# Loading q, k and v as f16 through GpSimd's DMA queue, with seven-product groups in chunks 3 to 5 and a new table of times

## The chip, the core and the metric

The kernel runs on one core of a Trainium2 chip. The metric is the time of one execution on the device in microseconds, in which smaller is better. The engines are called by the profile's names: PE (TensorE, matmuls), DVE (VectorE), ACT (ScalarE), POOL (GpSimd), SP (SyncE, which here only starts DMAs).

## The reference

Attention over 8 batches and 8 heads of 576 tokens, 64 numbers per head, without a softmax, followed by a two-layer network over all 4608 tokens.

```python
theta = np.pi / 2.0 * pos / S
def phi(x, c, s):
    r = np.maximum(x, 0.0)
    return np.concatenate([r * c, r * s], axis=-1)
q_p = phi(q, cos_w, sin_w); k_p = phi(k, cos_w, sin_w)
kv = np.einsum('bhsf,bhsd->bhfd', k_p, v)
z = np.sum(k_p, axis=2)
num = np.einsum('bhsf,bhfd->bhsd', q_p, kv)
den = np.einsum('bhsf,bhf->bhs', q_p, z)[..., None] + 1e-06
attn = num / den                       # then x: 4608 tokens x 512
h = x @ w_in                           # 512 x 2048
g = h * np.cos(h)
out = g @ w_out                        # 2048 x 512
```

Inputs and output are f32; PE multiplies f16.

## The kernel before

**Tiling.** The 576 tokens of a batch are four tiles of 128 and a rest of 64. The 64 left over from each batch are collected into a ninth piece of 512 tokens. So the network runs over nine chunks of 512 tokens: chunk c is batch c for c below 8, and chunk 8 holds the rests.

**Attention of a batch.** `load` brings q, k and v into `raw["q"]`, `raw["k"]`, `raw["v"]` (in the profile qm, km, vm; 128 partitions, 8 heads, 5 tiles, 64 numbers, f32) by two DMAs each, with 5 and with 4 tokens a piece (1280 and 1024 bytes). `prep` (L346 on ACT, L347 on DVE) takes the positive part, multiplies it with the cosine or sine of the position and writes f16 into `KQ`: 18 or 20 of these a batch. `cast_v` (L360, L361, L362) puts v in f16 into `V1` beside a column of ones. `kv` (L373) makes the 128 x 65 products of k and v for each head. q is transposed, for the first two batches on PE (`q_pe`, L402) and later by a DMA (`q_dma`, L412). `num` (L435, L451 to L455) multiplies, divides by the denominator and writes x in f16; x is transposed on PE (L475) or by a DMA (L485).

**Layer 1 of a chunk** multiplies 512 tokens with the 512 x 2048 weights and applies h cos(h). Chunks 0 and 1 do it in halves of tokens (L529). From chunk 2 on there are four groups of four column blocks each. A plain group (`layer1_plain`, L561) has 16 matmuls of 512 columns into four PSUM banks, and for each bank `gate`: a cosine on ACT (L502) and a multiply on DVE (L504). A seven-product group (`layer1_fast`, L667) makes the same result by a scheme of Strassen's kind, from sums of tokens' halves (`layer1_sums`, L624) and sums of weights (`w_in_sums`, L603): seven products of four matmuls of 256 columns. Partial results are put together outside PE: three copies on ACT (L675) and three adds on DVE (L679) into the f32 tiles Y, U and Z, a `gate` for Y and one for the bank that ends last, and `out2`, a double cosine (L690) and a double multiply (L696) over U and Z together. Gates of Y and double multiplies may run on DVE or POOL.

`FAST1 = {3:2,4:2,5:2,6:4,7:4,8:4}` (L568) says how many of a chunk's four groups are of the seven-product kind: none in chunk 2, two in chunks 3 to 5, all in 6 to 8.

**Layer 2** (`layer2`, L861, for chunks from 1 on; `layer2_plain`, L786, for chunk 0) is a seven-product scheme over the whole chunk. Its results go through the f32 tiles `ost` (L872, L883) to the output by `store`: DMAs from POOL's queue (L732, L749), some of them adding to what lies there (L745, L819).

**The order.** Nothing is scheduled while the kernel runs. Each piece of work is added to `Plan` as a step with what it reads and writes. `Plan.run` sorts all 1363 steps by a table of times, `STARTS` (units of 10 ns), and puts each on the engine that the string `ENGS` names (P, A, D, G for POOL, S for SP). Each engine runs its steps in that order, and a step waits for the semaphores of what it needs. So a step that waits holds up all that stands behind it on its engine. Steps marked `port=True` (preparations, casts of v, multiplies with a choice of DVE and POOL, sums between SBUF tiles) wait for each other across DVE and POOL as well, in the order of the table:

```python
if s["port"] and s["on"] in "DG":
    if last is not None and last[0] != s["on"]:
        tc.add_manual_dep(ins.ins, last[1].ins.name, SYNC, reason="shared port")
    last = (s["on"], ins)
```

**The queues.** SP starts the loads of q, k and v and the transposing DMAs. POOL starts the loads of the weights, which cast f32 to f16 on the way, and the stores, beside its own casts and multiplies. ACT starts two loads of constants and some of the last stores.

In the first stages 28 and then 17 matmuls on constant data (`warm`, L945) fill PE's time until batch 0 has arrived. In the last two chunks the tiles of q, k and v are free, and `layer1_fast` uses them as further buffers for Y, U, Z and for the sums of tokens.

Of the kernel before, what the change touches and what calls it, by code (L numbers as in the profile page):

```python
# [16 lines left out]

STARTS = (
# [166 lines left out]
def kernel(  # L185
# [42 lines left out]
    def sb(name, shape, dt=F16):  # L228
        return pool.tile(shape, dt, name=name)
# [897 lines left out]
```

## Time and profile before

| | |
|---|---|
| runs of the kernel | 281.53, 282.29 and 1005.16 us, median 282.29 |
| span of the profiled execution, first to last instruction | 279.7 us |
| busy in the span: PE, DVE, ACT, POOL | 97%, 85%, 75%, 30% |
| granted PE clock | full (1.000) |
| DMA moved | 58.03 MB, 207 GB/s over the span |
| SP's queue, POOL's queue: bytes moved | 39.99 MB, 17.04 MB |
| chain that ended last: PE, ACT, DVE | 92%, 3%, 2% |
| PE's matmuls by part: layer 2 (L861), layer 1 in sevens (L667), plain (L561), halves (L529) | 896, 504, 160, 256 |

The median of the runs is 2.6 us above the profiled span. "Busy" counts an engine's instructions and not the DMAs that it starts, save on POOL, where the writing of descriptors shows as busy. The time of a group of instructions is given as the mean of one; matmuls follow each other closer than their own length, since they are pipelined.

### The profile page before, as it was taken

Reading aid. Unit: us, or ns where it says so; the run is one execution under the profiler, and the core shown is the slowest. Engines: PE = TensorE matmul, PEld = TensorE weight load, DVE = VectorE, ACT = ScalarE, POOL = GpSimd, SP = SyncE. Lnnn points to the kernel's source line nnn. Section 1 sums busy time; section 2 is a strip of 40 time slices with the busy share of each in tenths; the row PEclk is TensorE's granted clock in tenths of the full one; section 3 lists DMA queues with packets and bytes.
Section 4 is the critical chain, followed back from the end, with each engine's and each line's share of the span. In section 5 each row is a group of like instructions: output and inputs, shape, how many; then the busy total and the mean of one; then the engine's idle time right before and its main releaser. Section 6 shows DMA issues by size and latency. Waiting matters only on the chain.

```text
span 279.7 us, 6825 instructions
## 1 busy us (share of the span) xinstructions
PE 272.6 (97%) x2698; PEld 215.5 (77%) x2698; DVE 236.9 (85%) x442; ACT 210.2 (75%) x363; POOL 82.9 (30%) x102
## 2 busy tenths in 40 slices
PE   8999999999999999999999999999999999999993
PEld 2567857787966677769777878789988888888882
DVE  1767698989999999999999998989989879873952
ACT  2756699879998897788989988995758686776330
POOL 1430020030501201520340045132534372399210
PEclk9999999999999999999999999999999999999999
DMA  6999989999999999989999998549756495698125
GB/s 207 312 202 206 340 239 241 361 301 174 335 261 271 258 249 246 234 268 259 255 258 246 242 229 284 98 115 141 163 75 139 110 156 105 152 143 123 75 77 150
DMA packets 80223, 58.03 MB, mean 207 GB/s; under 512 B 43200, under 2 KB 77248, under 8 KB 80192
## 3 DMA queue, kind: packets, MB, share of 16 engines
q1 hardware_dynamic: 68960, 39.99, 59.4%
q0 software_dynamic: 10496, 17.04, 30.1%
q10 hardware_dynamic: 736, 0.57, 0.7%
q8 instruction: 21, 0.34, 0.5%
q14 instruction: 10, 0.08, 0.1%
HBM read 36.75 MB, written 11.80 MB: 174 GB/s over the span
## 4 chain that ended last, share of the span: by engine, by line
PE 92%; ACT 3%; DVE 2%; issue 1%; POOL 0%; ACTq 0%; POOLq 0%
PE M L861 34%; PE M L667 14%; PE M L561 11%; PE M L529 9%; PE TR L667 6%; PE ATT L945 5%; PE ATT L435 3%; PE M L786 3%; PE ATT L373 3%; PE TR L561 2%; ACT KQ L346 2%; DVE x L455 1%; PE M L402 1%; PE M L373 0%; PE TR L475 0%
## 5 line engine op out<-in xcount | busy, mean ns | idle before, releaser
L861 PEld LDWEIGHTS <-gT 128*128 128x128 f16 x560 | 53.9, 98 | 8.3
L861 PE MATMUL M<-w_out_sb,gT 128*128 128x256 f16 x448 | 57.1, 273 | 0.0
L504 DVE TENSOR_TENSOR gT<-M,ch 128x512 f16<-128x512 f32 x73 | 48.5, 685 | 5.9 <-ACT ch L502 5.7
L502 ACT ACTIVATE ch<-M 128x512 f32<-128x512 f32 x75 | 43.4, 596 | 12.0 <-PE M L529 5.4
L346 ACT ACTIVATE KQ<-km,CS 128x512 f16<-128x512 f32 x57 | 38.5, 717 | 1.4 <-DMA km<-in_k_dram 1.3
L872 ACT ACTIVATE ost<-M 128x512 f32<-128x512 f32 x41 | 24.3, 596 | 17.9 <-PE M L861 13.0
L346 ACT ACTIVATE KQ<-qm,CS 128x512 f16<-128x512 f32 x46 | 31.5, 720 | 4.1 <-DMA qm<-in_q_dram 4.1
L561 PE MATMUL M<-xT,w_in_sb 128*128 128x512 f16 x136 | 33.8, 379 | 0.0
L861 PE MATMUL M<-T,S 128*128 128x256 f16 x256 | 32.4, 273 | 0.0
L667 PEld LDWEIGHTS <-w_in_sb 128*128 128x128 f16 x288 | 27.3, 98 | 4.8 <-issue 0.3
L362 POOL CAST V<-vm 128x1024 f16<-128x1024 f32 (+1 forms) x18 | 15.9, 907 | 50.8 <-DVE den L451 20.7
L529 PE MATMUL M<-xT,w_in_sb 128*128 128x256 f16 x256 | 30.3, 273 | 0.3 <-DVE gT L504 0.3
L861 PEld LDWEIGHTS <-S 128*128 128x128 f16 x256 | 24.8, 98 | 4.1 <-DVE S L837 0.2
L529 PEld LDWEIGHTS <-w_in_sb 128*128 128x128 f16 x256 | 24.4, 98 | 3.9 <-issue 0.5
L679 DVE TENSOR_TENSOR Z<-M,Z 128x512 f32<-128x512 f32 x31 | 21.1, 687 | 4.3 <-PE M L667 3.1
L561 PEld LDWEIGHTS <-w_in_sb 128*128 128x128 f16 x160 | 14.9, 98 | 12.2
L504 POOL TENSOR_TENSOR gT<-Z,ch 128x512 f16<-128x512 f32 x5 | 6.3, 1268 | 56.6 <-ACT ch L502 20.0
L455 DVE TENSOR_TENSOR x<-ATT,rec 128x512 f16<-128x512 f32 x32 | 22.1, 691 | 1.1
L435 PEld LDWEIGHTS <-qT 128*128 128x128 f16 (+1 forms) x320 | 14.8, 101 | 5.6 <-issue 3.5
L690 ACT ACTIVATE ch<-Z 128x1024 f32<-128x1024 f32 x12 | 12.7, 1057 | 6.9 <-DVE Z L679 4.8
L675 ACT ACTIVATE Z<-M 128x512 f32<-128x512 f32 x26 | 15.1, 596 | 3.4 <-PE M L667 2.4
L435 PE MATMUL ATT<-kvz,qT 128*128 128x65 f16 (+1 forms) x288 | 16.0, 195 | 0.8 <-DVE x L455 0.5
(150 smaller groups left out, 519.3 us busy)
## 6 DMA issues: line engine op xcount, KB each, us to landing
out_dram<-ost POOLq DMA_DIRECT2D x38, 256.0 KB, 4.3
qm<-in_q_dram SPq DMA_DIRECT2D x8, 640.0 KB, 6.7
km<-in_k_dram SPq DMA_DIRECT2D x8, 640.0 KB, 7.1
qm<-in_q_dram SPq DMA_DIRECT2D x8, 512.0 KB, 6.0
km<-in_k_dram SPq DMA_DIRECT2D x8, 512.0 KB, 6.0
vm<-in_v_dram SPq DMA_DIRECT2D x6, 640.0 KB, 5.7
vm<-in_v_dram SPq DMA_DIRECT2D x6, 512.0 KB, 4.6
w_in_sb<-in_moe_w_in_dram POOLq DMA_DIRECT2D x4, 512.0 KB, 8.8
```

The source lines that it names most:

```text
L346: fn = {"ACT": lambda: nc.scalar.activation(out=out_, in_=in_, func=AF.Relu, scale=sc), "DVE": lambda: nc.vector.tensor_scalar(out=out_, i ...
L362: "POOL": lambda: nc.gpsimd.tensor_copy(out=out_, in_=in_)}
L435: nc.tensor.matmul(bank[hb][ps, hh * D1:(hh + 1) * D1], lhsT=x[:, h, :], rhs=z[:, h, :], start=True, stop=True)
L455: nc.vector.tensor_tensor(out=split(x16[n][:, hs, :], k), in0=A[:, :, :, 0:D], in1=split(rec[n][:, hs], k).unsqueeze(3).broadcast_to((P, k ...
L502: act(0.5, due, lambda: nc.scalar.activation(out=ch[c], in_=bank, func=AF.Sin, bias=math.pi / 2.0, scale=1.0), [key], [("ch", c)])
L504: mul(due, 0.61, lambda q: q.tensor_tensor(out=dst, in0=bank if len(dst.shape) == 2 else bank.rearrange("p (j s) -> p j s", j=dst.shape[1] ...
L529: nc.tensor.matmul(M1[m][:, jj * 2 * P:(jj + 1) * 2 * P], lhsT=w_in_sb[:, cc, j * P:(j + 1) * P], rhs=X[:, cc, ts], start=(cc == 0), stop= ...
L561: nc.tensor.matmul(M, lhsT=w_in_sb[:, cc, j * P:(j + 1) * P], rhs=X[:, cc, :], start=(cc == 0), stop=(cc == NCT - 1))
L667: nc.tensor.matmul(bank[0][:, j * TH:(j + 1) * TH], lhsT=a(cc, j), rhs=b[:, cc, :], start=(first and j == 0 and cc == 0), stop=(last and j ...
L679: dve(0.61, due + 0.3, lambda: nc.vector.tensor_tensor(out=dst, in0=bank[0], in1=dst, op=ALU.add), [bank[1], key], [key])
L861: nc.tensor.matmul(bank[0][:, tt * MH:(tt + 1) * MH], lhsT=a[:, j, tt * P:(tt + 1) * P], rhs=b[:, j, :], start=(first and (apart or tt == ...
L872: act(0.5, due, lambda: nc.scalar.activation(out=dst, in_=view(bank), func=AF.Copy), [bank[1]], dk)
```

## The change

The tiles of q, k and v become f16, and the DMAs that load them, now on POOL's queue, cast on the way. The plain stores go to SP's queue; the adding ones stay on POOL's. Casts of v in batches 2 to 7 may run on DVE. `FAST1` is 4 for chunks 3 to 8. Outside the last two chunks U and Z have two buffers instead of one; in these they have five, and the sums of tokens get a second set of tiles of their own. Y has one buffer throughout, where it had four in the last two chunks. `STARTS` and `ENGS` are new and have 1405 steps. In the new `ENGS`, 19 double multiplies instead of 5 run on POOL, and 63 preparations instead of 49 on DVE (89 instead of 103 on ACT).

The diff holds further code that does not run with these settings (`MODE` is empty): another form of `layer1_fast`, in which a bank is written instead of an f32 tile, and the notes in `full` on which it depends. It is left out here, and so are the two tables.

```diff
+OPT = dict(F16=1, FAST1={3: 4, 4: 4, 5: 4, 6: 4, 7: 4, 8: 4}, MODE={}, HH=0, W2=0, SQ=1, NUZ=2)
...
-    raw = {nm: sb(f"{nm}m", [P, H, NT + 1, D], F32) for nm in "kqv"}
+    raw = {nm: sb(f"{nm}m", [P, H, NT + 1, D], F16 if OPT["F16"] else F32) for nm in "kqv"}
...
+    LQ, LE, LO = (nc.gpsimd, "POOL", 0.9) if OPT["F16"] else (nc.sync, "SP", 0.65)
+    FD = 0.16 if OPT["F16"] else 0.30
...
             def go5(h=h, five=five):
-                nc.sync.dma_start(out=blocks(m, n)[:, h], in_=five)
+                LQ.dma_start(out=blocks(m, n)[:, h], in_=five)
 
             def go4(h=h, four=four):
-                nc.sync.dma_start(out=blocks(m, 1 - n)[:, h, 0:NT, :], in_=four)
+                LQ.dma_start(out=blocks(m, 1 - n)[:, h, 0:NT, :], in_=four)
...
-            pl.add("SP", 0.65, 0, due, go4, (), [(x, 1 - n) for x in part], dma=(nb * NT, 355.0),
+            pl.add(LE, LO, 0, due, go4, (), [(x, 1 - n) for x in part], dma=(nb * NT, 355.0),
...
-        either(due, {e: cost[e] for e in ([eng] if eng else VCAST)}, fn, rd, wr)
+        either(due, {e: cost[e] for e in ([eng] if isinstance(eng, str) else eng)}, fn, rd, wr)
...
-    FAST1 = {3:2,4:2,5:2,6:4,7:4,8:4}
+    FAST1 = OPT["FAST1"]
...
-    Z3 += [flat(raw[nm], F32)[:, 0:3 * SM] for nm in "kqv"]
-    Z3UZ = [z[:, SM:3 * SM] for z in Z3]
-    Z3 = [[z[:, i * SM:(i + 1) * SM] for i in range(3)] for z in Z3]
-    XSS += [[flat(raw["k"])[:, 6 * SM + i * SM:6 * SM + (i + 1) * SM].rearrange(
-        "p (c s) -> p c s", c=CH2) for i in range(4)]]
+    if F16IN:
+        XSS += [[sb(f"XT{i}", [P, CH2, TH]) for i in range(4)]]
+        uz = [Z3[0][:, SM:3 * SM]] + [sb(f"UZ{i}", [P, 2 * SM], F32) for i in range(OPT["NUZ"] - 1)]
+        NUZ = len(uz)
+        uz += [flat(raw[nm], F32)[:, 0:2 * SM] for nm in "kqv"]
...
+    Z3UZ = uz
+    YS = [Z3[0][:, 0:SM]] + ([] if F16IN else [flat(raw[nm], F32)[:, 0:SM] for nm in "kqv"])
...
-        st_ = zn[0] % 4 if c >= B - 1 else 0
+        st_ = zn[0] % (len(Z3UZ) if c >= B - 1 else NUZ)
...
+            Y = YS[st_ % len(YS)]
+            U, Z = Z3UZ[st_][:, 0:SM], Z3UZ[st_][:, SM:2 * SM]
...
-                    pl.add("POOL", 0.55, 0, due, lambda dst=dst, src_=src_: nc.gpsimd.dma_start(out=dst, in_=src_),
+                    SQ, SE, SO = (nc.sync, "SP", 0.62) if OPT["SQ"] else (nc.gpsimd, "POOL", 0.55)
+                    pl.add(SE, SO, 0, due, lambda dst=dst, src_=src_, SQ=SQ: SQ.dma_start(out=dst, in_=src_),
                            keys, [("out", c, h, i)], dma=(kb, 355.0))
...
-            put(due, five[:, 2 * h:2 * h + 2, :], blocks(O, n), keys, nc.gpsimd, "POOL")
-            put(due, four[:, 2 * h:2 * h + 2, :], blocks(O, 1 - n), keys, nc.gpsimd, "POOL")
+            Q = (nc.sync, "SP") if OPT["SQ"] else (nc.gpsimd, "POOL")
+            put(due, five[:, 2 * h:2 * h + 2, :], blocks(O, n), keys, *Q)
+            put(due, four[:, 2 * h:2 * h + 2, :], blocks(O, 1 - n), keys, *Q)
...
-            cast_v(b, t, "POOL", T + 6 + 0.4 * t, nt=nt)
+            cast_v(b, t, ("POOL", "DVE") if OPT["F16"] else "POOL", T + 6 + 0.4 * t, nt=nt)
```

More of the change, by code (lines that the diff above doesn't have):

```diff
@@ L134 @@
-    "SASAAPPDSADSA"
+    "DDPGGGGGGGGGGGGGGGGDAPDDDPADAPDDAPAPDADADDDADADADADDADADPPADPPDPPAPPDPPAPPDPPAPPDPAPADPA"
+    "DPADPADPADPADPADPADPADPADPADPADPADPADPADPADGGGGGGGGGGGGGGGDADADADADADAPDDAPADAPDDAPADADA"
+    "DADDADADPPAPPDPAPPDPAPPDPAPPDPAPDPPDPAPAPAPAPAPDPDSSPDPDSSPADPADPADPADPADPADPADPADPADPAD"
+    "PADPADPADPADPADPADDDDDGGGGGGAAAAADDDAAGGGPPAAASADSDASAASPPDPAPPDPAPPDPAPPDPADDDPPAPPDDPP"
+    "APPAPPDPPDSSPPASSPADPADPADPADPADPADPADPADPADPADPADPADPADPADPADPADGGGGGGDADDAADDDADGDPPAA"
@@ new lines @@
+    "ASDASDASDASADPPDSPPDSPPDSPPDSSPPDSDDDDDDDDDDDPPAPPDDPPAPPAPPDPPDSSPPASSDDDDPAPDAGPAPAPDP"
+    "DAGPADPAPDAGPAPAPDPDAGPADPAPDADPAPAPDPDAGPADPAPDAGPAPAPDPDAGPADGGGGGGDDDAAADAADGDDPPAAAS"
+    "DDSAASDASPPDSPPDSPPDSPPDSDDDPPAPPDDPPAPPAPPDPPDSSPPASSDDDDPAPDADPAPAPDPDAGPADPAPDAGPAPAP"
+    "DPDAGPADPAPDAGPAPAPDPDAGPADPAPDADPAPAPDPDAGPADGGGGGGAADDAAADADGGGPPADASAASDASAASAAPPDSPP"
+    "DSPPDSPPDSSPPDSDDDPPAPPADPPASSPPAPPAPPAGGPPASSGGDDDDPAPDAGPAPAPDPDAGPADPAPDAGPAPAPDPDAGP"
+    "ADPAPDADPAPAPDPDAGPADPAPDADPAPAPDPDAGPADGGGGGGAADDAADAADGDGPPAADSAASAASADSPPDSPPDSPPDSPP"
@@ L135 @@
+    "DSDDDPPAPPADPPASSPPAPPAPPAGGPPASSGGDDDDPAPDAGPAPAPDPDADPADPAPDADPAPAPDPDAGPADPAPDAGPAPAP"
+    "DPDAGPADPAPDADPAPAPDPDADPADGGGGGGAAAADAAAAAGGDPPADASAASDASDDSDDPPDSPPDSPPDSPPDSSPPDSDDSP"
+    "PAPPAGGPPASSPPAPPAPPAGGPPASSGGDDDDPAPDADPAPAPDPDAGPADPAPDADPAPAPDPDADPADPAPDADPAPAPDPDAG"
+    "PADPAPDAGPAPAPDPDADPADDDDDSPPAPPDGGPPAPPAPPDPPDSSPPASSDDDDPAPDADPAPAPDPDAGPADPAPDADPAPAP"
+    "DPDAGPADPAPDADPAPAPDPDAGPADPAPDAGPAPAPDPDADPADDDDDDDPPAPPDDDPPAPPAPPDPPDSASAAPPDSADSA"
 )
@@ L344, in prep @@
         f = len(heads) / H
-        cost = {"DVE": 0.09 + 0.33 * f, "ACT": 0.12 + 0.5 * f}
+        cost = {"DVE": 0.09 + FD * f, "ACT": 0.12 + 0.5 * f}
         fn = {"ACT": lambda: nc.scalar.activation(out=out_, in_=in_, func=AF.Relu, scale=sc),
@@ L358, in cast_v @@
         f = nt * len(heads) / H
-        cost = {"DVE": 0.09 + 0.33 * f, "ACT": 0.12 + 0.5 * f, "POOL": 0.1 + 0.5 * f}
+        cost = {"DVE": 0.09 + FD * f, "ACT": 0.12 + 0.5 * f, "POOL": 0.1 + 0.5 * f}
         fn = {"ACT": lambda: nc.scalar.activation(out=out_, in_=in_, func=AF.Copy),
@@ L362, in cast_v @@
               "POOL": lambda: nc.gpsimd.tensor_copy(out=out_, in_=in_)}
-        either(due, {e: cost[e] for e in ([eng] if eng else VCAST)}, fn, rd, wr)
+        either(due, {e: cost[e] for e in ([eng] if isinstance(eng, str) else eng)}, fn, rd, wr)
+    full = {}
     def kv(b, due, pair=None):
@@ L378, in kv @@
             hs = range(hb * HB, (hb + 1) * HB)
+            full[keys[hb]] = False
             pe(HB * (NT + 1), MMA, due, lambda hb=hb: mm(hb),
@@ L403, in mm @@
                                  rhs=IDENT, is_transpose=True)
+        full[key] = False
         pe(H, MMT, due, mm, [("qp", t, g, h) for g in range(2) for h in range(H)] + ["ID"], [key])
@@ L438, in num @@
         for hb in range(2):
+            full[keys[hb]] = False
             pe(HB * len(parts), MMA, due, lambda hb=hb: mm(hb), rd, [keys[hb]])
@@ L476, in mm @@
                                  is_transpose=True)
+        full[key] = False
         pe(NCT, MMT, due, mm, [("x16", n), "ID", *after], [key])
@@ L532, in mm @@
                                         start=(cc == 0), stop=(cc == NCT - 1))
+                        full[("M1", m)] = False
                         pe(2 * NCT, MMH, due, mm, xk[2 * hf:2 * hf + 2] + [("w_in", quarter)],
@@ L562, in mm @@
                                  start=(cc == 0), stop=(cc == NCT - 1))
+        full[mk] = True
         pe(NCT, MM, due, mm, xk + [("w_in", j // 4)], [mk])
@@ L577 @@
     LATE = min(c for c, nf in FAST1.items() if nf > 2)
-    assert all(FAST1[c] == NJT // 4 for c in range(LATE, NC))
     def flat(t, dt=F16):
@@ L582, in flat @@
             "p a b c d -> p (a b c d)")
-        return v if dt == F32 else v.bitcast(F16)
+        return v.bitcast(dt)
     WSB = {1: w_in_sb[:, 0:CH2, 3 * JF:4 * JF]}
@@ L586 @@
         WSB[n] = sb(f"WSB{n}", [P, CH2, JF])
+    F16IN = OPT["F16"]
     Z3 = [sb("Z3", [P, 3 * SM], F32)]
     XSS = [[sb(f"XS{i}", [P, CH2, TH]) for i in range(4)]]
-    Z3 += [flat(raw[nm], F32)[:, 0:3 * SM] for nm in "kqv"]
-    Z3UZ = [z[:, SM:3 * SM] for z in Z3]
-    Z3 = [[z[:, i * SM:(i + 1) * SM] for i in range(3)] for z in Z3]
-    XSS += [[flat(raw["k"])[:, 6 * SM + i * SM:6 * SM + (i + 1) * SM].rearrange(
-        "p (c s) -> p c s", c=CH2) for i in range(4)]]
+    if F16IN:
[3 more added lines that the diff above has]
+        uz += [flat(raw[nm], F32)[:, 0:2 * SM] for nm in "kqv"]
+    else:
+        uz = [Z3[0][:, SM:3 * SM]]
+        NUZ = 1
+        uz += [flat(raw[nm], F32)[:, SM:3 * SM] for nm in "kqv"]
+        XSS += [[flat(raw["k"])[:, 6 * SM + i * SM:6 * SM + (i + 1) * SM].rearrange(
+            "p (c s) -> p c s", c=CH2) for i in range(4)]]
+    Z3UZ = uz
+    YS = [Z3[0][:, 0:SM]] + ([] if F16IN else [flat(raw[nm], F32)[:, 0:SM] for nm in "kqv"])
+    ZX = [Z3[0][:, i * SM:(i + 1) * SM] for i in range(3)]
     def w_in_sums(f, due):
@@ L641, in layer1_fast @@
         XS = XSS[i]
-        A, Bk = next_bank(3), next_bank(3)
-        st_ = zn[0] % 4 if c >= B - 1 else 0
+        A, Bk = next_bank(c), next_bank(c)
+        st_ = zn[0] % (len(Z3UZ) if c >= B - 1 else NUZ)
         zn[0] += 1
-        Y, U, Z = Z3[st_]
-        zk = [("Z3", st_, n) for n in range(3)]
+        mode = OPT["MODE"].get(c, "Y")
+        fork = mode in "FX" and full.get(Bk[1], False)
+        if mode == "X":
+            st_ = zn[0] % 3
+            Z = ZX[st_]
+            zk = [None, None, ("ZX", st_)]
+            Y, zk[0] = (ZX[(st_ + 1) % 3], ("ZX", (st_ + 1) % 3))
+            alias = []
+        else:
+            Y = YS[st_ % len(YS)]
+            U, Z = Z3UZ[st_][:, 0:SM], Z3UZ[st_][:, SM:2 * SM]
+            zk = [("Y", st_ % len(YS))] + [("Z3", st_, n) for n in range(1, 3)]
+            alias = ["AL"] if st_ >= NUZ else []
+        full[A[1]] = full[Bk[1]] = True
         j0 = 2 * g
@@ L675, in copy @@
             act(0.5, due + 0.3, lambda: nc.scalar.activation(out=dst, in_=bank[0], func=AF.Copy),
-                [bank[1]] + (["AL"] if st_ else []), [key])
+                [bank[1]] + alias, [key])
         def plus(dst, bank, key, due):
@@ L705, in layer1_fast @@
         d = product(A, -11, b11, xk, True, False)
-        copy(Y, A, zk[0], d)
-        d = product(Bk, -12, b21, xk, True, True)
-        plus(Y, Bk, zk[0], d)
-        out(Y, zk[0], 0, 0, d, c in Y_POOL)
+        if fork:
+            act(0.5, d + 0.3, lambda: nc.scalar.activation(out=Bk[0], in_=A[0], func=AF.Copy),
+                [A[1]], [Bk[1]])
+            d = product(Bk, -12, b21, xk, False, True)
+            out(Bk[0], Bk[1], 0, 0, d)
+        else:
+            copy(Y, A, zk[0], d)
+            d = product(Bk, -12, b21, xk, True, True)
+            plus(Y, Bk, zk[0], d)
+            out(Y, zk[0], 0, 0, d, c in Y_POOL)
+        if mode == "X":
+            d = product(Bk, 1, XS[0], [("XS", i, 0)], True, False)
+            copy(Z, Bk, zk[2], d)
+            d = product(A, 2, XS[1], [("XS", i, 1)], False, False)
+            dve(0.61, d + 0.3, lambda: nc.vector.tensor_tensor(
+                out=Bk[0], in0=A[0], in1=Z, op=ALU.add), [A[1], zk[2]], [Bk[1]])
+            d = product(Bk, 4, b22, xk, False, True)
+            out(Bk[0], Bk[1], 0, 1, d)
+            d = product(A, 3, XS[2], [("XS", i, 2)], False, False)
+            plus(Z, A, zk[2], d)
+            out(Z, zk[2], 1, 1, d, True)
+            d = product(A, -22, XS[3], [("XS", i, 3)], False, True)
+            out(A[0], A[1], 1, 0, d)
+            return
         d = product(A, 2, XS[1], [("XS", i, 1)], False, False)
```

17 lines of the change are left out of this document (1 added, 16 removed), and 199 rows, old and new, of the table STARTS.

## The prediction

> **What bounds the kernel now.** I read the page's busy times first, then the windows of the steady stages, then the chain that ended last, then the DMA issues.
>
> ```profile
> span 279.7 us, 6825 instructions
> PE 272.6 (97%) x2698; PEld 215.5 (77%) x2698; DVE 236.9 (85%) x442; ACT 210.2 (75%) x363; POOL 82.9 (30%) x102
> PE   8999999999999999999999999999999999999993
> POOL 1430020030501201520340045132534372399210
> ```
>
> TensorE is busy in every slice but the first and the last. A busy PE need not be PE at its peak, so I look at the pace of its matmuls in the chain:
>
> ```profile
> 79.51 2.59 PE M L561 x12
> 216.58 1.31 PE M L667 x12
> 1.32 9.04 PE ATT L945 x28
> 11.25 3.67 PE ATT L945 x17
> 15.37 1.22 PE M L373 x40
> ```
>
> Columns: start, length, what. Twelve plain layer-1 matmuls of 512 columns take 2.59, or 0.216 each; twelve matmuls of a seven-product group (256 columns) take 1.31, or 0.109 each. Half the columns, half the time, no gap: PE runs at its column rate. The last three rows are the start: 28 and then 17 filler matmuls until the loads and preparations of batch 0 allow the k-v products at 15.4. Chain and page agree that PE makes up 92% of the path.
>
> ```profile
> 80.00:107.00 27.00, 27.00 (x253) 18.21 (x252) 26.34 (x50) 23.60 (x42) 2.60 (x3) 1.00 1.17 244
> 107.00:134.00 27.00, 27.00 (x267) 21.29 (x266) 25.98 (x48) 21.81 (x38) 7.30 (x9) 1.00 1.02 254
> 134.00:161.00 27.00, 27.00 (x286) 21.39 (x284) 25.68 (x48) 24.70 (x44) 5.99 (x8) 1.00 1.06 247
> 161.00:188.00 27.00, 27.00 (x267) 21.33 (x266) 24.59 (x45) 23.46 (x42) 10.61 (x13) 1.00 0.80 178
> ```
>
> Columns: stretch, its length, busy PE, PEld, DVE, ACT, POOL, clock, DMA share, GB/s. The last three rows are the stages of chunks 3, 4 and 5. PE has no idle time to win back there, the clock is full, and DVE stands at 91 to 96% with ACT behind it at 81 to 91%. So a gain can come only from PE work that goes away, and it is kept only if DVE, ACT and GpSimd keep pace.
>
> **The change, part by part.**
>
> *Chunks 3 to 5.* Six plain groups become seven-product groups. A plain group is 16 matmuls of 0.216 = 3.45; a seven-product group is 28 of 0.109 = 3.06. Saved: 0.39 x 6 = 2.4 us, all on the path. It is paid on the other engines. Each converted group drops four cosines (ACT 0.60) and four multiplies (DVE 0.69) and adds, by the rows of the groups already there, three copies (ACT 0.60), three adds (DVE 0.69), two cosines (0.60), a double cosine (1.06), two multiplies (0.69) and a double multiply (DVE 1.22, GpSimd 2.35). ACT: +1.65 a group, +9.9 in three stages. DVE: +1.9 a group, +11.5, if nothing moves; 3 x 27 - 76.3 = 4.7 is free there. So the moves decide.
>
> *What the new tables move* (counted in both tables, whole kernel). Fourteen more double multiplies go to GpSimd (19 instead of 5), eight fewer run on DVE. Fourteen preparations go from ACT (0.72) to DVE, six of GpSimd's casts of v go to DVE. ACT: -24 x 0.60 + 18 x 0.60 + 12 x 0.60 + 6 x 1.06 - 14 x 0.72 = -0.1 us, even. DVE: -24 x 0.69 + 18 x 0.69 + 11 x 0.69 - 8 x 1.22 = -6.3, plus six casts (about +2, at 0.28 for 256 elements) and the preparations, 49 before and 63 after. GpSimd: +14 x 2.35 + 1 x 1.27 for multiplies, 52 loads, -32 plain stores x 0.56, -6 casts x 0.9.
>
> *f16 preparations on DVE.* No row of before has one. A preparation from f32 (512 elements) is 0.48, a cast of 256 elements is 0.28. That gives 0.08 fixed and 0.40 for 512 elements; half of the latter gives 0.28. Bounds: 0.28, and 0.48 for no gain at all. I take 0.30: 63 x 0.30 - 49 x 0.48 = -4.6, so DVE goes down by some 9 us and the +11.5 is met by what left. At 0.48 it would be +6.7 and DVE some 2 us up, still inside its free time over the kernel (42.8 us) but not in the stages of chunks 2 to 4. On the path: 0 either way if the order holds; up to +2 at 0.48.
>
> *Loads on GpSimd's queue.*
>
> ```profile
> L956 POOL DMA_DIRECT2D w_in_sb<-in_moe_w_in_dram x4: 750/862/1008, 11.1 to 13.8; - x4
> L970 POOL DMA_DIRECT2D w_out_sb<-in_moe_w_out_dram x4: 742/746/926, 17.7 to 39.2; - x4
> L819 POOL DMA_DIRECT2D gT<-S x2: 1585/1774/1963, 221.3 to 245.8; - x2
> out_dram<-ost POOLq DMA_DIRECT2D x38, 256.0 KB, 4.3
> out_dram<-ost SPq DMA_DIRECT2D x1, 256.0 KB, 3.2
> ```
>
> The first three rows are durations (least, median, most, ns) of GpSimd's issues. The weight loads cast f32 to f16 as the new loads do, with the same 512 pieces each; they hold GpSimd for 0.74 to 1.01. The dear bound is the accumulating transfer of 1024 pieces, 1.77. I take 0.87: 52 x 0.87 = 45 us of GpSimd, where SP spent 0.6 on each. The transfers themselves: f32 loads moved 340 to 390 GB/s in the first 10 us, the weight loads about 200 GB/s counted in f16, which is 400 of f32. So the time in the DMA engines stays as it is, cost 0. Landing takes 4.3 from GpSimd's queue against 3.2 from SP's: +1.1 for each load, hidden by loads that are issued a stage ahead, except at the start.
>
> The Trainium skill has a rule against this: "SBUF — State Buffer", the box on "DVE blocks DMA" (SWDGE), says that GpSimd can't write descriptors while VectorE is in a two-port mode. Here the four L956 issues, beside preparations and casts from f32 on DVE, took 0.75 to 1.01 and the median of L970, with few of these beside it, 0.75; so the trace shows at most 0.26 for it. By the rule an issue would wait for whole DVE instructions; for the sum that changes nothing until GpSimd is full, which is the rival below.
>
> *The start.* q is first issued at 0.74 on SP and prepared from 7.23. On GpSimd it follows two memsets that end at 1.48, and lands 1.1 later: preparations from 7.23 + 0.74 + 1.1 = 9.1. The f16 preparations are shorter on DVE, but ACT's three take 1.95: transposes at about 11 where PE's fillers end at 10.4. The new order puts a third transpose before the second fillers, so these still end at 10.36 + 3 x 0.45 + 3.67 = 15.4, as now; v's last part lands 1.8 later than now, at 15.5, and the second half of the k-v products waits for it. Bounds: 0 (everything under the fillers) and +1.8. I take +0.4.
>
> *Stores on SP.* SP loses 52 loads x 0.6 and gains 32 stores x 0.62; a store that waits for its tile holds back the transposing DMAs queued behind it (q and x, 50 of them), which feed attention a stage later. Cost 0; if the cover were gone, the length of one such wait, up to 4 us by the longest that GpSimd's stores waited (L732 for ACT, 4.0).
>
> *Buffers.* The layer-1 result Y has one buffer in the last two chunks instead of four, U and Z two before that instead of one. ACT copies that would wait sit beside DVE at 75% or less there. I allow +0.2 for all new hand-overs between GpSimd and ACT.
>
> **Sum.** 279.7 - 2.4 + 0.4 + 0.2 = 277.9 of span. The median run is 2.6 above the profiled span (282.3 against 279.7), so 280.5 us.
>
> **The rivals.** *All of it and the start too (about 279.3).* f16 preparations shorten the DVE chain before the first layer-1 matmul and nothing waits: 282.3 - 2.4 - 0.6. For: DVE's casts and preparations lie in that chain's first part. Against: the loads come later.
>
> *The gain is spent in chunks 2 to 5 (283.5).* Five engines at 90% or more in one order: each late copy holds a PSUM bank and PE waits. With f16 preparations at 0.48 (+2 on the path) and 12 double multiplies in these stages handed over at 0.1 each, 3.2 us go: 282.3 - 2.4 + 0.4 + 3.2 = 283.5, about as before. For: DVE at 95%. Against: of all that waited for today's double multiplies (L696), ACT's double cosine lost most, 2.6 us in three waits, and PE nothing. The Trainium skill ("VectorE: DVE Perf Modes", the perf-mode tier table) has f16 `tensor_scalar` at 4x where f32 has 2x, which speaks against this case; no run here shows it yet.
>
> *GpSimd becomes the bound (289, slower).* In the 30 us that the new table gives to chunk 3, GpSimd has ten loads (8.7), four double multiplies (9.4), three single ones (3.8) and five casts (4.3): 26.2. There is room for 0.38 a load. It decides from 1.25 us a load on. At 1.77, the dear row, it is 26.2 + 9.0 - 30 = 5 us over in this stage, and some 3 in the next with two loads, four double multiplies and longer multiplies beside descriptor writing (3.75 instead of 2.35 has been seen once, in chunk 8 behind two L819): 282.3 - 2.4 + 0.4 + 8.5 = 288.8. Late loads then make late preparations on ACT and DVE, and PE waits for both. For: multiplies, loads and casts stand in one queue. Against: the cast loads of before never took more than 1.01.
>
> **How the numbers follow.** Forecast 0.60; more gain 0.10; gain spent 0.15; GpSimd bound 0.15. The forecast's own range is 279.3 to 282.3. To hold 8 in 10 the range must take in the spent gain and part of the last rival: 278.3 to 287.5. A difference of 2% (5.6 us) is about what a measurement of this kernel can tell from no change. Faster than 276.7 would need more than all of the PE work removed: 0.03. Slower than 287.9 is most of the GpSimd rival: 0.12. Within: 0.85.
>
> **What would show it.** Right: 42 more L667 products and 96 fewer plain matmuls at the same 0.109 and 0.216, PE at 27.0 of 27 between 80 and 269, span down by about 2; f16 preparations near 0.30; cast loads near 0.87. The start is right if the k-v products begin at 15.4 to 16. Wrong: PE below 26 of 27 in the windows from 107 to 161, with ACT or DVE waiting for GpSimd's double multiplies, or preparations waiting for DMA; loads above 1.25; first layer-1 matmuls after 23.

## The result, and the profile after

The changed kernel takes 315.7 us (314.4 to 318.3) where the kernel before takes 281.9 beside it: 1.121 times as long, 95% interval 1.115 to 1.127. The forecast was 280.5 with a range up to 287.5; all three rivals that it named stay below 290. For three of the kernels below the runs lie more than 1.5% apart, and of these only the runs near the fastest are held against other kernels.

The page of the changed kernel: busy times, and PE and its granted clock in 40 slices of a span of 314.2 us.

```profile
PE 281.8 (90%) x2770; PEld 225.5 (72%) x2770; DVE 230.8 (73%) x459; ACT 211.9 (67%) x361; POOL 130.3 (41%) x131
PE   8999998974998957994999989999999999997994
PEclk9999999995999997998799999999999999999999
```

No engine has become the bound: DVE, ACT and GpSimd are all further from full than PE. PE has holes, and the large ones lie in slices 8 to 23, counted from 0, that is from 63 to 188 us. The windows of that part, with the columns of the prediction's windows (the last three are clock, DMA share, GB/s):

```profile
60.00:80.00 20.00, 13.25 (x139) 10.25 (x137) 11.97 (x29) 10.01 (x18) 6.21 (x8) 0.83 1.28 176
80.00:107.00 27.00, 25.90 (x264) 19.11 (x263) 24.84 (x53) 21.68 (x38) 8.11 (x11) 1.00 1.28 152
107.00:134.00 27.00, 21.24 (x213) 15.80 (x212) 19.46 (x38) 15.81 (x28) 4.35 (x6) 0.94 0.95 153
134.00:161.00 27.00, 22.70 (x238) 19.14 (x237) 19.04 (x43) 16.92 (x30) 15.70 (x14) 0.87 1.33 188
161.00:188.00 27.00, 24.09 (x276) 20.40 (x274) 23.18 (x48) 23.01 (x40) 14.86 (x12) 1.00 0.95 115
```

PE is busy for 107.2 of the 128 us from 60 to 188. Before, it was busy for all 128:

```profile
60.00:188.00 128.00, 128.00 (x1323) 99.07 (x1321) 120.78 (x221) 112.69 (x197) 31.26 (x40) 1.00 1.03 240
```

In the rows with the largest holes the granted clock is lower too (0.83, 0.94, 0.87), and its mean over this stretch is 0.93. So, as an estimate, the stretch holds about 107.2 x 0.93 = 99.7 us of work at full clock, some 28 us less than before: most of the 34 that were lost. In the first row every engine is idle for a third of the time or more, and the DMA share is at 1.28 (a share above 1 means that records of packets overlap on an engine). What PE waited for (the view of waits, PE only: us in total, times, longest), the five largest rows:

```profile
PE ATT L448 <- DMA qT<-KQ: 13.0, 6, 6.6
PE M L577 <- DVE gT L519: 4.2, 1, 4.2
PE M L705 <- ACT Z L713: 2.1, 2, 1.5
PE M L921 <- ACT ost L932: 1.6, 2, 1.4
PE TR L705 <- DMA xT<-x: 1.6, 1, 1.6
```

The second row goes back to a transposing DMA too: just before it DVE, whose multiply PE lacks, stood still for the transposed x (all waits, the row of L650):

```profile
DVE XS L650 <- DMA xT<-x: 5.4, 1, 5.4
```

Before, PE's list has four rows and no DMA of any kind in them. This is the largest:

```profile
PE ATT L945 <- POOL S L931: 1.3, 1, 1.3
```

`qT<-KQ` is the transposing DMA that turns a tile of prepared q for the numerator products. It did not change, and SP still issues it. The view of tile qT between 50 and 190 us says how long these DMAs take from issue to landing. Before, then after:

```profile
DMA to landing us min/median/max: 3.0/5.3/8.2
```

```profile
DMA to landing us min/median/max: 3.0/6.2/13.5
```

The best case is the same, 3.0 us. The bad ones are not, and the four issued between 60 and 80 us took 12.3 us in the median. PE's order is fixed in advance, so one late tile stops everything behind it.

### The profile page after: what moved, and what is told of

The parts are those of the page before. It is cut to its first block, busy times and chain, and to the rows that moved or that the text cites. A ratio compares the mean times of both kernels' runs of the same rounds, so it can differ in the third digit from the quotient of the medians.

```text
span 314.2 us, 7016 instructions
## 1 busy us (share of the span) xinstructions
PE 281.8 (90%) x2770; PEld 225.5 (72%) x2770; DVE 230.8 (73%) x459; ACT 211.9 (67%) x361; POOL 130.3 (41%) x131
## 5 line engine op out<-in xcount | busy, mean ns | idle before, releaser
L517 ACT ACTIVATE ch<-M 128x512 f32<-128x512 f32 x60 | 35.5, 595 | 18.5 <-DVE gT L519 6.9
L519 DVE TENSOR_TENSOR gT<-M,ch 128x512 f16<-128x512 f32 x58 | 39.4, 686 | 9.6 <-ACT ch L517 8.8
L705 PEld LDWEIGHTS <-w_in_sb 128*128 128x128 f16 x384 | 37.1, 99 | 8.4 <-issue 3.4
L355 ACT ACTIVATE KQ<-qm,CS 128x512 f16<-128x512 f16 x43 | 29.2, 720 | 11.3 <-issue 7.7
L355 ACT ACTIVATE KQ<-km,CS 128x512 f16<-128x512 f16 x46 | 31.0, 718 | 3.1 <-DMA km<-in_k_dram 3.1
L717 DVE TENSOR_TENSOR Z<-M,Z 128x512 f32<-128x512 f32 x42 | 27.9, 685 | 3.9 <-ACT Z L713 2.8
L371 POOL COPY V<-vm 128x1024 f16<-128x1024 f16 (+1 forms) x12 | 11.2, 946 | 36.5 <-DVE den L465 21.9
L734 POOL TENSOR_TENSOR gT<-UZ,ch 128x1024 f16<-128x1024 f32 x8 | 19.3, 2413 | 11.8 <-DVE gT L519 6.3
L734 POOL TENSOR_TENSOR gT<-Z,ch 128x1024 f16<-128x1024 f32 x7 | 16.5, 2364 | 13.1 <-DVE XS L650 8.1
L577 PE MATMUL M<-xT,w_in_sb 128*128 128x512 f16 x64 | 16.9, 399 | 4.2 <-DVE gT L519 4.2
L519 POOL TENSOR_TENSOR gT<-Z,ch 128x512 f16<-128x512 f32 x10 | 13.7, 1367 | 16.4 <-DVE gT L734 6.5
```

The lines of the kernel that those rows point to most:

```text
L355: fn = {"ACT": lambda: nc.scalar.activation(out=out_, in_=in_, func=AF.Relu, scale=sc), "DVE": lambda: nc.vector.tensor_scalar(out=out_, i ...
L517: act(0.5, due, lambda: nc.scalar.activation(out=ch[c], in_=bank, func=AF.Sin, bias=math.pi / 2.0, scale=1.0), [key], [("ch", c)])
L519: mul(due, 0.61, lambda q: q.tensor_tensor(out=dst, in0=bank if len(dst.shape) == 2 else bank.rearrange("p (j s) -> p j s", j=dst.shape[1] ...
L705: nc.tensor.matmul(bank[0][:, j * TH:(j + 1) * TH], lhsT=a(cc, j), rhs=b[:, cc, :], start=(first and j == 0 and cc == 0), stop=(last and j ...
L717: dve(0.61, due + 0.3, lambda: nc.vector.tensor_tensor(out=dst, in0=bank[0], in1=dst, op=ALU.add), [bank[1], key], [key])
L734: mul(due, 1.14, lambda q: q.tensor_tensor(out=g4, in0=four(uz), in1=four(cc2), op=ALU.mult), [zk[1], zk[2], *ck], [("g", gi(c), h * JH + ...
```

## The experiments

The theories as the expectations number them. **1 (later A, and 1a with bursts of loads):** the transposing DMAs share the DMA engines with the loads' new queue, and land late. **2:** the cast costs the DMA engines time. **3:** stores on SP's queue hold the transposing DMAs up. **4:** the new table, its seven-product groups and GpSimd's multiplies have no slack. **B:** the new table leaves a transposing DMA less time than it takes undisturbed. **C:** the order is at fault in that it was made for landings that it doesn't get.

### The transfers by themselves

A small kernel with eight stages of loads, transposing DMAs and stores.

> The disputed transfers by themselves, nothing of the attention or the MoE is computed and out is written in part only. Eight stages, each opened when all of the stage before has landed: (1) four transposing DMAs alone; (2) six f32 loads of one batch on SP; (3) six cast loads on GpSimd's queue; (4) six f32 loads on SP and four transposing DMAs behind them in the same queue; (5) two transposing DMAs ahead of two loads, twice, all on SP; (6) six f32 loads on GpSimd's queue and the four transposing DMAs on SP at once; (7) the same with cast loads; (8) as 7 with two stores ahead of the transposing DMAs on SP. Theory 1 (two queues share the DMA engines): a transposing DMA lands in about 3 us in stage 1 and in the front pair of stage 5, and in 8 to 14 us in stages 6 and 7 alike, though nothing stands ahead of it on SP. Theory 2 (the cast costs the engines time): stage 3 lasts at least 1.2 times stage 2, and a transposing DMA is late in stage 7 but not in stage 6. Theory 3 (stores on SP's queue hold the transposing DMAs up): stage 7 lands them in 3 to 5 us and stage 8 4 us or more later.

Stages 3 and 4 ran into each other, and stage 8 began inside stage 7. Stages 1 and 6 are read here. Alone, a transposing DMA landed after 3.3 us (stage 1). Beside six f32 loads on GpSimd's queue (stage 6, tile QT):

```profile
L61 SPq DMA_TRANSPOSE QT<-QS x4: 1244/3102/7143, 80.8 to 92.5; - x4
DMA to landing us min/median/max: 5.3/9.5/13.9
```

Nothing stood ahead of them on SP, so theory 1 holds beside f32 loads. The first row is new too: the issuing instruction itself, 1.3 us in stage 1, held SP for up to 7.1.

The second version waits for everything before it opens a stage.

> The transfers by themselves again, with stages that cannot overlap; nothing of the attention or the MoE is computed and out is written in part only. Stages: (1) six f32 loads of one batch on SP; (2) six cast loads on GpSimd's queue; (3) six f32 loads on GpSimd's queue; (4) four transposing DMAs alone; (5) SP alone: two f32 loads, two transposing DMAs, four loads, two transposing DMAs; (6) six cast loads on GpSimd's queue beside four transposing DMAs on SP; (7) the same with two stores ahead on SP; (8) two cast loads on GpSimd's queue beside four transposing DMAs. Theory A (a transposing DMA gets one of its many 256 B packets through for each packet of the loads' queue): (4) lands them 1.4 us apart, (6) about 5.8 us apart as long as loads last (64 packets of 21 ns and 70 ns by turns on each engine), so the second and third land 9 us or more after issue, in (8) only the first is late, and in (5) the first pair lands 6 us after issue however many loads follow. Theory 2 (the cast costs the engines time): (2) lasts 1.2 times (1), by the packets' 69 and 60 ns against 55 and 46 ns; more than 1.3 times would make it a cause of its own. Theory 3 (stores): (7) lands them 3 us or more later than (6).

Six f32 loads on SP, six cast loads on GpSimd's queue and six f32 loads there took 12.9, 12.4 and 13.4 us from the first issue to the last landing. So the cast makes the loads no slower by themselves, and theory 2 falls. The four transposing DMAs alone (stage 4), with the stage's queue row, in a window of 8 us:

```profile
q1 hardware_dynamic: 4224, 1.05, 68.4%
...
QT<-QS SPq DMA_TRANSPOSE x4, 3.3
```

The same four beside six cast loads (stage 6), tile QT:

```profile
L61 SPq DMA_TRANSPOSE QT<-QS x4: 1233/2610/4939, 82.5 to 89.3; - x4
DMA to landing us min/median/max: 5.8/10.3/12.6
```

The first row of stage 4 gives the price: 4224 packets in 68.4% of 16 engines x 8 us are 21 ns each, 66 packets on each engine for one transposing DMA, 1.4 us. That is also the distance of their landings in stage 4. The cast loads' stage has 3168 packets at 96.1% of 13.5 us, 66 ns each. If the engines take the two queues packet by packet, a transposing DMA needs 66 x (21 + 66) ns = 5.7 us; the landings in stage 6 (at 88.3, 93.5 and 98.1) are 5.2 and 4.6 apart, a tenth and a fifth less. The packets that began between the first two of these landings (the queue rows of the window from 88.3 to 93.5; the loads are in q0, the transposing DMAs in q1):

```profile
q0 software_dynamic: 1156, 0.65, 89.8%
q1 hardware_dynamic: 1152, 0.29, 45.8%
```

The Trainium skill ("DMA: Bandwidth & Descriptors", "Queues, rings and completion order") says that each DMA engine goes round between the queues it has work for, a packet at a time; the two equal counts agree with it. A small packet then pays for a large one each turn. The sum comes out high because the two shares add up to 1.36, so that packets of the two queues overlap. For the long packets of f32 loads on GpSimd's queue equal turns are too dear a rule: 864 packets at 75.7% of 14 us are 196 ns each, which would make 14.3 us of a transposing DMA, and the first two landings beside them were 7.8 apart. Between these two (88.2 to 96.1 us of the first small kernel) 1858 packets of SP's queue went beside 505 of the loads, so there the turns are not one record against one; what they are stays open.

In one queue (stage 5) the two behind two loads landed 5.6 and 5.1 us after issue, though four more loads followed. With only two cast loads (stage 8) it was 5.9, 7.3, 6.6 and 3.1, where only the first was expected to be late. With two stores ahead on SP (stage 7) the four landed 11.3, 14.9, 10.9 and 6.4 us after issue, against 5.8, 9.7, 12.6 and 10.9 in stage 6: the first two 5 us later. From the first one's issue to the last one's landing it is 18.4 us against 17.7, so the stores delay the front of the row and hardly the whole.

### The parts of the change on the kernel before

```diff
-                nc.sync.dma_start(out=blocks(m, n)[:, h], in_=five)
+                nc.gpsimd.dma_start(out=blocks(m, n)[:, h], in_=five)
...
-            pl.add("SP", 0.65, 0, due, go5, ...
+            pl.add("POOL", 0.9, 0, due, go5, ...
```

(and `go4` alike), still f32, with the table and the order of the kernel before:

> The kernel before, its table and its order untouched, with the loads of q, k and v issued by GpSimd instead of SP, still f32. Theory 1 (two queues): SP's queue holds the transposing DMAs alone, they share the DMA engines with a backlog of loads, land after 8 to 13 us instead of 3 to 8 us and hold PE up: 292 to 315 us, with idle time of PE at L435 put down to DMA qT<-KQ. Theory 2 (the cast is what costs): 280 to 284 us, since nothing is cast. Theory 3 (stores on SP) and theory 4 (the new table and its seven-product groups have no slack): 280 to 284 us.

310.9 us, 1.104 times before (1.098 to 1.109). The loads' queue alone costs 28 us, with no cast, no new table and no stores moved. Theory 1 holds. With the cast added (`raw` in f16, the tiles kept large enough for what else lives in them):

> The kernel before with the loads of q, k and v on GpSimd's queue and cast to f16 there; table, groups and stores as before. Theory 1 (two queues): as with the f32 loads on GpSimd's queue, within 5 us of that run, 292 to 315 us. Theory 2 (the cast): 15 us or more above that run. Theory 4 (the new table): 280 to 284 us, the preparations on DVE being 0.1 to 0.2 us shorter each.

290.3 us, 1.028 (1.025 to 1.031): 21 us better than without the cast, where theory 1 had expected the same and theory 2 worse. The pages show one thing in which the two differ. Row q0 of the f32 kernel, then of the f16 kernel:

```profile
q0 software_dynamic: 17472, 45.36, 59.8%
```

```profile
q0 software_dynamic: 35904, 31.20, 69.2%
```

2.6 KB a packet against 0.87, over all that the queue carries. The longest landing of qT between 50 and 190 us is 17.9 us in the first and 12.0 in the second. PE waits 17.8 us for qT in the first and 5.6 in the second. That the longer packets are the whole reason is not shown: preparations from f16 are shorter as well, and in the small kernels four transposing DMAs took as long beside the one as beside the other (16.9 us from the first issue to the last landing beside f32 loads, 17.7 beside cast loads).

```diff
-                    pl.add("POOL", 0.55, ... nc.gpsimd.dma_start(out=dst, in_=src_),
+                    pl.add("SP", 0.62, ... nc.sync.dma_start(out=dst, in_=src_),
...
-            put(due, five[...], blocks(O, n), keys, nc.gpsimd, "POOL")
+            put(due, five[...], blocks(O, n), keys, nc.sync, "SP")
```

> The kernel before with its plain stores issued by SP instead of GpSimd, loads and transposing DMAs in SP's queue as before. Theory 3 (a store that waits for its sums holds back the transposing DMAs behind it): 295 us or more, with idle time of PE put down to DMA qT<-KQ or xT<-x. Theories 1, 2 and 4: 281 to 286 us.

282.4 us, 1.000 (0.998 to 1.003). Stores on SP cost the old kernel nothing that can be measured.

### Taking parts out of the changed kernel

The old table with the same queue and cast loses 8 us, the new one 34. Five kernels look for the other 26.

```diff
-OPT = dict(..., SQ=1, NUZ=2)
+OPT = dict(..., SQ=0, NUZ=2)          # stores on GpSimd's queue
```

> The changed kernel with its plain stores back on GpSimd's queue; loads cast on GpSimd's queue, table and groups as changed. The kernel before with the cast loads alone went to 290 us, so some 25 us of the change's loss are not yet placed. Theory 1a (two queues, and the new table puts three and four loads at once beside a transposing DMA where the old one has one or two): 311 to 320 us. Theory 3 (once the loads are gone from SP's queue, it is the stores that hold the transposing DMAs up there): 288 to 296 us. Theory 4 (the new table and its seven-product groups have no slack, whatever the transfers do): 311 to 320 us.

315.6 us, 1.117 (1.114 to 1.120), the same as with stores on SP. Theory 3 is out in this kernel too.

```diff
+        LQ, LE, LO = (nc.gpsimd, "POOL", 0.9) if nm == "v" else (nc.sync, "SP", 0.65)
```

(in `load`, with `raw` for q and k in f32, and the second set of sums of tokens back in k's tile):

> The changed kernel with q and k loaded by SP as f32, in one queue with the transposing DMAs again; v is still cast on GpSimd's queue, stores on SP, table and groups as changed. Preparations on DVE then read f32, 0.1 to 0.2 us longer each. Theory 1a (two queues and the bursts of loads beside the transposing DMAs): the loss goes with the loads' queue, 280 to 288 us. Theory 4 (the new table has no slack): 300 us or more. Theory 3 (stores on SP): 295 us or more.

A miss: 314.7 us at best, 321.8 at worst, no gain on the changed kernel. By the expectation that speaks for theories 3 and 4. But the run traded one lateness for another: PE's waits for qT fall to 7.4 us, while PE is busy for 51.0 us of the first 60 instead of 56.2, and ACT and DVE wait for km and qm (10.7 and 8.0 us on ACT, 8.6 and 6.9 on DVE). The new order has loads and transposing DMAs side by side, and here they stand in one queue again. So the run does not separate the theories.

```diff
+            if s["kind"] == "turn":
+                turn = ins
+            if s["kind"] == "load" and turn is not None:
+                tc.add_manual_dep(ins.ins, turn.ins.name, SYNC, reason="behind the transpose")
```

(the two kinds are set where the steps are added)

> The changed kernel with one wait more: each load on GpSimd's queue waits until the transposing DMA ahead of it in the table has landed, so that a transposing DMA meets only loads issued before it, as in one queue. Theory 1a: a transposing DMA lands within 8 us again, and PE's waits for qT and xT shrink to a third: 284 to 300 us, what is left being loads that start late and GpSimd's own work behind the wait. Theory 4 (the new table has no slack): 311 us or more. Theory 3 (stores on SP): 305 us or more.

321.5 us, 1.141 (1.134 to 1.147): worse than the change itself, a second miss. The median landing of qT did come down, to 4.3 us. The price is in the waits:

```profile
DVE WSB L630 <- POOL gT L520: 11.5, 2, 7.7
ACT KQ L356 <- DMA qm<-in_q_dram: 11.2, 3, 8.0
POOL vm L331 <- DMA xT<-x: 9.8, 1, 9.8
ACT ch L729 <- POOL gT L735: 9.3, 2, 8.8
```

GpSimd stands waiting to issue vm (third row). Behind that wait are the next loads, whose preparations ACT then lacks (second row), and GpSimd's own multiplies, which DVE and ACT lack (first and last row).

```diff
         pl.add("SP", 1.25, 0, due, lambda: nc.sync.dma_start(
-            out=dst, in_=qp[:, t]..., transpose=True),
+        pl.add("SP", 1.25, 0, due, lambda: None,
```

(in `q_dma`, and the same in `x_dma`):

> The changed kernel without the transposing DMAs of batches 2 to 7: the products read what stood in their tiles before, all other work and all other waits stay. Theory 1a (late transposing DMAs are the whole loss): 278 to 283 us, the table is kept. Theory 4 (the new table, its seven-product groups, GpSimd's multiplies have no slack): 295 us or more.

289.0 us, 1.022 (1.017 to 1.027). 27 of the 34 us are gone, so they are tied to the transposing DMAs. 6 to 7 are not, which neither theory had. GpSimd issues all loads here and does all its multiplies, so it is not GpSimd's own time that cost the 27.

```diff
-                LQ.dma_start(out=blocks(m, n)[:, h], in_=five)
+                LQ.dma_start(out=blocks(m, n)[:, h][:, 0:HB if b > 1 else None],
+                             in_=five[:, 0:HB if b > 1 else None])
```

(and `go4` alike):

> The changed kernel whose loads of batches 2 to 7 bring heads 0 to 3 only (heads 4 to 7 keep what stood there): the same instructions, queues, order and table, half the bytes and packets beside the transposing DMAs. Theory A (the loads of the other queue hold the transposing DMAs up): most of the loss goes, 285 to 295 us. Theory B (the new table leaves a transposing DMA less than the 3.3 us that it takes undisturbed, so that it stalls PE whatever else is in flight): 302 us or more.

288.9 us, 1.025 (1.023 to 1.027). All transposing DMAs are there, at their places in the new table, and half the bytes beside them are enough to take away the same 27 us. So it is neither the transposing DMAs nor the table's room for them alone (theory B falls), but the two transfers on the same engines. qT landed after 4.7 us in the median, 8.9 at most.

### The order

> The changed kernel with the same steps and transfers in another order, on each engine (and a few preparations, casts and multiplies on another of their engines): the order is made by letting the steps run, on paper, with the transfers as the traces show them (a cast load 32 packets of 70 or 61 ns on each DMA engine, a transposing DMA 64 or 32 of 21 ns, one packet of each busy queue in turn), which puts the changed kernel's own order at 309 us and the order made here at 284. Theory A with C (the queues make the transposing DMAs late, and the new table was made for landings that it doesn't get; an order that allows for them recovers most): 283 to 295 us. If the DMA engines are simply too full for any order: 305 us or more.

301.9 us, 1.068 (1.062 to 1.075): 14 us better than the change, not the 284 of the paper, and between the two ranges. It lost at the start, where PE is busy for 49.5 of 60 us against 56.2; what the paper had wrong there is not shown. Two further orders leave the changed kernel's start alone.

> As the first reordering (the changed kernel's steps and transfers, an order worked out on paper with landings as the traces show them), but the changed kernel's own order is kept for all steps that its table puts before 50 us; on paper 283 us, with loads a twentieth faster 280, a twentieth slower 293. Theory A with C (late landings, and an order that was not made for them): 279 to 291 us, and the waits for qT all but gone. Theory 4 (the seven-product groups and GpSimd's multiplies themselves): 300 us or more, since they are all still there.

> A second order from another start of the same search, with the changed kernel's own order kept up to 56 us; on paper 285 us, with loads a twentieth slower 295. Theory A with C: 281 to 293 us. Theory 4: 300 us or more.

296.4 us, 1.050 (1.046 to 1.054), for the first, which misses its range by 5 us. The second took 290.5 us at best, inside its range, and 295.7 to 297.2 in its three other runs, outside it; no ratio is given. Both are under the 300 that theory 4 asked for. The steps, the groups, the bytes and the queues are those of the changed kernel, and no step is gone; in the first of the two 76 of the 1405 steps run on another of the engines DVE, ACT and GpSimd. The order with these moves gives 19 us back, and how much of it the moves alone would give was not tried. PE from 60 to 188 us in the first of the two:

```profile
60.00:188.00 128.00, 122.73 (x1319) 101.64 (x1318) 113.72 (x225) 108.42 (x189) 59.48 (x53) 1.00 1.13 161
```

122.7 busy instead of 107.2, at full clock and with the DMA share as high as before. The wait for qT is gone from PE's list. PE still lacks 5.3 us in this stretch, and 5.9 more between 188 and 260, where the kernel before has no hole; its largest wait is now for output copies (L902 for ost L913, 4.9 us).

### What is left without transfers in the way

> The changed kernel with loads of batches 2 to 7 for heads 0 to 3 only and without the transposing DMAs of these batches (the products read what stood there before). Each of the two alone left 287 to 290 us. If what is left is still transfers in each other's way: 280 to 283 us. If it is the new order and its steps, in the first 60 us and at the end: 286 to 290 us.

286.5 us, 1.016 (1.013 to 1.020), in the second range: the last 5 us are not loads and transposing DMAs in each other's way. PE's waits in this run, its five largest:

```profile
PE M L919 <- ACT ost L930: 2.0, 2, 1.4
PE M L542 <- DVE gT L517: 1.8, 2, 1.3
PE ATT L1004 <- POOL S L989: 1.3, 1, 1.3
PE M L703 <- ACT Z L711: 0.5, 1, 0.5
PE TR L488 <- DVE den L464: 0.5, 1, 0.5
```

Only the third row is in the kernel before. The rest are hand-overs in the first layer 1 (L542 for gT) and at the end (L919 for ost).

The runs side by side, qT landings (median and longest) and PE's busy time both from the middle stretch:

| Kernel | us | qT to landing, 50 to 190 us | PE busy of 128, 60 to 188 us |
|---|---|---|---|
| before | 281.9 | 5.3, 8.2 | 128.0 |
| before, stores on SP | 282.4 | 5.7, 8.4 | 127.1 |
| before, cast loads on GpSimd's queue | 290.3 | 6.9, 12.0 | 121.5 |
| before, f32 loads on GpSimd's queue | 310.9 | 8.5, 17.9 | 106.7 |
| changed | 315.7 | 6.2, 13.5 | 107.2 |
| changed, stores on GpSimd's queue | 315.6 | 7.2, 15.2 | 109.4 |
| changed, q and k loaded by SP | 314.7 at best | 5.3, 10.4 | 110.2 |
| changed, loads wait for transposing DMAs | 321.5 | 4.3, 11.6 | 104.1 |
| changed, half the loads | 288.9 | 4.7, 8.9 | 125.5 |
| changed, second order | 296.4 | 4.8, 10.5 | 122.7 |
| changed, half the loads, no transposing DMAs | 286.5 | none | 127.5 |

With one order and nothing else made late, PE's time falls as the landings get longer, if not evenly: on the changed kernel a median of 7.2 costs no more than one of 6.2. The two kernels in which loads are late for other reasons do not fit. Between orders it does not follow from the landings alone: the old table with the cast loads has a median of 6.9 and loses 6.5 us of PE, the new one has 6.2 and loses 20.8. By the two tables, in the part from 45 to 190 us, the time from a transposing DMA's place to the place of the first step on any engine that must wait for it is never under 5.3 us in the old one; in the new one it is under 4.5 for nine of 50, and 2.6 at least. That this is what makes the new order the more fragile is argued from the tables; that the order, with its placing on engines, can take most of it away is shown by the reordered runs.

## Why the prediction was wrong

**What bounds the kernel.** Right: PE's order sets the end, and only PE work that goes away could be a gain. The other side of it was not drawn: with no idle time, anything late for PE is lost in full.

**Chunks 3 to 5.** The counts came as worked out (L705 has 672 matmuls against 504, the plain L577 has 64 against 160) at the same paces. Whether the 2.4 us were had can't be told: PE's busy time without transfers in the way is 272.3 against 272.6, and that time models the ends of matmuls. The 2.6 us added for a run above its span was too much: runs of the kernel before that list both are 1.8 to 2.2 above.

**The moves and f16 preparations.** No engine became full, as forecast. A preparation from f16 on DVE took 0.35 (median of 63), between the 0.30 taken and the 0.48 of f32, so a quarter less and not half. GpSimd's double multiplies took 2.35 in the largest group (2.35 forecast), single ones up to 3.1.

**Loads on GpSimd's queue: the step that failed.** The issue was mis-sized in the kind direction: 0.69 in the median instead of 0.87, below the weight loads' 0.74 to 1.01, so the GpSimd rival had no ground. The Trainium skill's rule on "DVE blocks DMA" ("SBUF — State Buffer") can hardly be seen in these 52 issues: they took 0.62 to 0.91, and all but three at most 0.73. That the transfers take the same time was right as far as it went (12.4 us for six against 12.9). The term that is missing stands in the next sentence of the prediction: landing "+1.1 for each load, hidden by loads that are issued a stage ahead". It asked who waits for the loads. It did not ask what else is in the queue that they leave. SP's queue had held loads and transposing DMAs in turn; with the loads gone to another queue, a transposing DMA shares the engines with everything that GpSimd has issued. The rows were there: 50 transposing DMAs on SP, 2.4 to 8.2 us to landing, a DMA share of 0.8 to 1.17 in the middle windows. The term was put at nothing. On the old table this term is 8 us with the cast and 28 without; on the new one 27.

**The start.** The k-v products began at 15.2 and the first layer-1 matmuls at 21.3, as before (15.2 and 21.2): the +0.4 was 0. The loads of batch 0 landed only 0.2 to 0.6 us later than before, the last part of v at 13.9 and not at 15.5. What was not in the sum comes later: without transfers in the way, layer 1 waits 1.8 us for gT.

**Stores on SP.** The cost of 0 is right in both kernels. The price without cover (one store that waits for its tile, up to 4 us) was not tested; two stores ahead that wait for nothing made the first two transposing DMAs of the small kernel 5 us later.

**Buffers.** +0.2 for "all new hand-overs between GpSimd and ACT" was too little for hand-overs of every kind: without transfers in the way, PE waits 5.3 us in all where the kernel before waits 1.0 (both without the 1.3 of the start), and the largest of these waits are for ACT's output copies and DVE's multiplies. These 4.3 us are most of the 6 between 286.5 and the forecast; the rest is not accounted for.

**The rivals.** "The gain is spent" looked at DVE and ACT, "GpSimd becomes the bound" at issue time. Both argue about engines; none was about two queues on the same DMA engines, and this is what happened. The "five engines at 90% or more" of the first are not in its rows, which have PE at 100%, DVE at 91 to 96, ACT at 81 to 91 and GpSimd at 10 to 39. One sign of being wrong did come, PE at 21.2 and 22.7 of 27 between 107 and 161, but with PE itself waiting for qT.

## What to carry to other kernels

Before a transfer is moved to another queue, list what stays behind in the old one and how soon each of these is needed: a queue's order is a priority, and the move gives it up. Price a transfer of small packets beside a busy second queue at (its packet + the other's packet) x its packets per engine, and not at its time alone: this was somewhat high here for the cast loads (5.7 us for 5.2 and 4.6) and almost twice too high for f32 loads. Give a fixed order that much room. A wait that restores the order costs whatever stands behind it on the engine that waits.

## What the runs showed of the hardware that was not expected

A transposing DMA of 256 KB, 1.4 us of DMA engine time and 3.3 us to landing alone, needed 4.6 to 5.2 us apiece beside cast loads on the other queue, and its issuing instruction held SP for up to 4.9 us (7.1 beside f32 loads) instead of 1.3. The six f32 loads that leave SP in 3168 packets leave GpSimd's queue in 864 (3.54 MB each time), which is hardly slower alone (13.4 us against 12.9 for six). The kernel took 311 us with them and 290 with the cast loads on the same queue. And the cast from f32 to f16 on the way made six loads no slower, 12.4 us.
